# Attention with a convolutional gated unit: row-tiled scores, masks on TensorE, PSUM copies regrouped, fourth-tap product on VectorE

## The chip, the cores and the metric

The kernel runs on one core of one Trainium2 chip. The metric is the device time of one execution in microseconds (us), median of several runs; the fast runs of a kernel mostly fell within 1.5% of each other. The engines are named as the profile names them: PE is TensorE (PEld its weight loads), DVE is VectorE, ACT is ScalarE, POOL is GpSimd, SP is SyncE, which issues transfers.

## The reference

Causal attention for 8 batches, 8 heads, 576 positions and head size 64, with a decay from a cumulative sum per head, followed by a gated unit whose gate is a causal convolution of five taps.

```python
scores = scale * np.matmul(q, k.transpose(0, 1, 3, 2))
s_pos = np.maximum(s, 0.0)
cum = np.cumsum(s_pos, axis=-1)
bias = -(cum[:, :, :, None] - cum[:, :, None, :])
scores = np.where(causal, -1000000000.0, scores + np.minimum(bias, 0.0))
...                                     # softmax
x = matmul(attn, v)                     # then (batch, 576, 512)
for k in range(K):                      # K = 5
    gate_pre += conv_w[k][None, None, :] * xp[:, k:k + S, :]
gate = 1.0 / (1.0 + np.exp(-gate_pre))
val = x @ w_val
return (gate * val @ w_out)
```

## The kernel before

The work is done by head pairs, four pairs a batch, 32 in all. For each pair: transposes of Q and K on TensorE, scores, exp on ScalarE, a triangle product for the mask on VectorE, the product with V on TensorE, normalisation (`xn`), a transpose back (`xT`), five taps of the convolution, tanh, the value matmul with the gate product (`glu`), and the output matmul. The two heads of a pair share the 128 partitions; so that one matmul sees one head alone, Q is written twice, each time with the other head's half left at zero (`QZ`).

```python
def load_v(b):                                   # once a batch, GpSimd, two inputs in SBUF
    Vp = sets[b % 2]["Vp"]
    for i in range(NKB):
        ...                                      # transfer of V into vst
        nc.gpsimd.tensor_tensor(Vp[:, i], vst[:, i], w[...], ALU.mult)

def qk_transpose(b, p, which):
    ...
    if which == 0:                               # Q: two zero-padded copies, VectorE
        for hh in range(2):
            r = slice(64 * hh, 64 * hh + 64)
            nc.vector.tensor_copy(st["QZ"][hh][r, p, 0:512].rearrange(...), pt[r, :].rearrange(...))
    else:                                        # K: ScalarE
        nc.scalar.copy(st["KT"][:, p, 0:512].rearrange("d (x j) -> d x j", j=4), ...)

def scores(b, p, step):
    ...
    for (kb, q0, nq, c0) in STEPS[step]:
        for hh in range(2):
            nc.tensor.matmul(ps[:, hh, c0:c0 + nq], st["KT"][:, p, kbo[kb]:kbo[kb] + 128],
                             st["QZ"][hh][:, p, q0:q0 + nq], start=True, stop=True)
    nc.scalar.activation(out=Pt[:, :, step * 512:(step + 1) * 512], in_=ps, func=AF.Exp, scale=0.125)
    if step == 0:                                # causal mask on the diagonal blocks, VectorE
        nc.vector.tensor_tensor(dg, dg, tri..., ALU.mult)

def conv(b, c):
    nc.scalar.activation(out=gp, in_=xc[:, 4:4 + S], func=AF.Copy, scale=cwT[...])   # fourth-tap product
    for kk in range(4):
        nc.vector.scalar_tensor_tensor(gp, xc[:, kk:kk + S], cwT[...], gp, ALU.mult, ALU.add)
    nc.scalar.activation(out=th, in_=gp, func=AF.Tanh, scale=0.5)
```

GpSimd also casts Q, K and their tails to bf16 for every batch (`qkb`, `tailb`). `psav`, the PSUM tile of the product with V, has one buffer.

## Time and profile before

| before | us |
|---|---|
| median time (runs 312.5 to 314.2) | 312.95 |
| span of the profiled run | 311.1 |
| first tap of the convolution starts | 45.6 |
| from there to the last glu: VectorE busy / idle | 238.8 / 13.9 |
| last glu to the end | 12.7 |

The last rows come from VectorE's timeline (where the first tap starts and the last glu ends) and from the windows view of the stretch between. The columns of that view are the window, its length, busy time and instruction count of PE, PEld, DVE, ACT and POOL, then the granted clock, the share of the transfers and GB/s.

### The profile page before, as it was taken

To read this page: it belongs to the slowest core of one execution; us is meant where nothing else is said; L and a number is where in the kernel's file an instruction comes from. 1 tells how busy PE (TensorE), PEld (TensorE's weight loads), DVE (VectorE), ACT (ScalarE), POOL (GpSimd) and SP (SyncE) were. 2 spreads that over 40 slices of the span, in tenths; PEclk is the share of its full clock that TensorE was granted. 3 is DMA by queue.
4 is the path that set the end of the run, shared out by engine and by line. 5 is a ranking of instruction groups with operands and counts; after the bars stand their busy time and mean duration, and the time that the engine had idled before them with its cause. 6 is when DMAs were issued, how large, how long until landed. Compare 5 with 4: busy or idle time off the path is not lost. (4 is left out here: it accounts for less than half of the span.)

```text
span 311.1 us, 6044 instructions
## 1 busy us (share of the span) xinstructions
PE 215.4 (69%) x2384; PEld 151.6 (49%) x2407; DVE 259.6 (83%) x456; ACT 186.4 (60%) x256; POOL 107.0 (34%) x88
## 2 busy tenths in 40 slices
PE   0273974596747686688678875889578888767880
PEld 0152763384525564565456553666365566433440
DVE  5060689999999999999998999989988999999710
ACT  0238885587636675587666774587457778534341
POOL 8992776900690019300860059001900000000000
PEclk9996796579895999799978997799959999997998
DMA  4999999986074016676774215301100021020243
GB/s 99 261 262 325 252 291 207 316 189 223 7 174 142 2 62 192 120 202 190 221 186 127 62 67 136 84 21 67 36 0 36 19 94 43 18 104 34 84 154 96
DMA packets 71925, 40.49 MB, mean 130 GB/s; under 512 B 49808, under 2 KB 66192, under 8 KB 71888
## 3 DMA queue, kind: packets, MB, share of 16 engines
q1 hardware_dynamic: 69008, 40.00, 47.2%
q8 instruction: 21, 0.34, 0.5%
q10 hardware_dynamic: 2880, 0.01, 0.5%
q14 instruction: 16, 0.13, 0.1%
HBM read 30.57 MB, written 9.44 MB: 129 GB/s over the span
## 5 line engine op out<-in xcount | busy, mean ns | idle before, releaser
L427 DVE SCALAR_TENSOR_TENSOR gp<-xT,cwT,gp 128x576 f32<-128x576 bf16 x128 | 123.7, 967 | 3.8 <-ACT gp L425 3.6
L379 ACT ACTIVATE P<-ps 128x1024 bf16<-128x1024 f32 x96 | 96.7, 1025 | 27.1 <-PE ps L377 24.2
L377 PE MATMUL ps<-QZ,KT 128*128 128x128 bf16 (+4 forms) x512 | 75.8, 273 | 16.9 <-ACT P L379 15.1
L314 POOL CAST qkb<-qkf 128x2048 bf16<-128x2048 f32 (+2 forms) x18 | 32.9, 1843 | 98.2 <-issue 44.1
L377 PEld LDWEIGHTS <-KT 128*128 128x128 bf16 x512 | 43.4, 110 | 32.4 <-issue 22.9
L395 PE MATMUL psav<-Vp,P 128*128 128x65 bf16 x960 | 43.6, 201 | 21.0 <-DVE xn L404 18.1
L325 POOL TENSOR_TENSOR Vp<-vst,w 128x520 bf16<-128x520 f32 x40 | 55.2, 1412 | 0.0
L395 PEld LDWEIGHTS <-P 128*128 128x128 bf16 x960 | 39.5, 103 | 27.7 <-issue 16.3
L440 PE MATMUL m<-xT,wv 128*128 128x288 bf16 x256 | 46.5, 314 | 7.1 <-DVE xT L419 4.4
L450 PE MATMUL m<-wo,glu 128*128 128x512 bf16 x137 | 40.2, 388 | 13.7 <-DVE glu L442 11.8
L453 ACT COPY ot<-m 128x512 f32<-128x512 f32 (+1 forms) x40 | 23.4, 585 | 37.0 <-PE m L450 35.0
L440 PEld LDWEIGHTS <-wv 128*128 128x128 bf16 x256 | 25.7, 106 | 20.9 <-issue 5.6
L430 ACT ACTIVATE th<-gp 128x576 f32<-128x576 f32 x32 | 21.9, 684 | 21.4 <-DVE gp L427 21.4
L442 DVE SCALAR_TENSOR_TENSOR glu<-th,m 128x288 bf16<-128x288 f32 x64 | 28.6, 448 | 6.6 <-PE m L440 6.1
L346 PE MATMUL m<-ident,qkb 128*128 128x128 bf16 x256 | 28.0, 242 | 6.9 <-DVE xT L419 3.3
L350 DVE COPY QZ<-m 64x512 bf16<-64x512 bf16 x64 | 26.8, 419 | 5.1 <-PE m L346 4.4
L450 PEld LDWEIGHTS <-glu 128*128 128x128 bf16 x160 | 15.7, 99 | 27.8 <-issue 16.6
L382 DVE TENSOR_TENSOR P<-P,tri 128x1024 bf16<-128x1024 bf16 x32 | 26.9, 841 | 2.8 <-ACT P L379 2.0
L425 ACT ACTIVATE gp<-xT,cwT 128x576 f32<-128x576 bf16 x32 | 24.8, 775 | 6.8 <-DVE xT L419 6.8
L404 DVE TENSOR_TENSOR xn<-psav,recs 128x640 bf16<-128x640 f32 x32 | 26.1, 815 | 0.1
L346 PEld LDWEIGHTS <-qkb 128*128 128x128 bf16 x256 | 19.4, 108 | 12.7 <-issue 7.5
L416 DVE COPY xT<-m 128x512 bf16<-128x512 bf16 x32 | 21.4, 668 | 0.7 <-PE m L415 0.7
(50 smaller groups left out, 134.2 us busy)
## 6 DMA issues: line engine op xcount, KB each, us to landing
vst<-in_v_dram SPq DMA_DIRECT2D x32, 256.0 KB, 4.8
out_dram<-ot SPq DMA_DIRECT2D x32, 256.0 KB, 2.0
qkf<-in_q_dram SPq DMA_DIRECT2D x7, 1024.0 KB, 6.6
qkf<-in_k_dram SPq DMA_DIRECT2D x7, 1024.0 KB, 8.6
tail<-in_q_dram SPq DMA_DIRECT2D x8, 128.0 KB, 3.9
tail<-in_k_dram SPq DMA_DIRECT2D x8, 128.0 KB, 3.9
vst<-in_v_dram SPq DMA_DIRECT2D x8, 128.0 KB, 3.8
qkf<-in_moe_w_val_dram SPq DMA_DIRECT2D x1, 1024.0 KB, 6.5
```

Source lines behind the costliest of these rows:

```text
L314: nc.gpsimd.tensor_copy(t.rearrange("p j (h d) -> p h j d", h=8)[:, h0:h1], f.rearrange("p h (j d) -> p h j d", j=4)[:, h0:h1])
L325: nc.gpsimd.tensor_tensor(Vp[:, i], vst[:, i], w[:, i, b * 8:(b + 1) * 8].unsqueeze(2).to_broadcast([128, 8, 65]), ALU.mult)
L346: nc.tensor.transpose(pt[:, j * 128:(j + 1) * 128], st["qk"][which][:, j, c], ident)
L350: nc.vector.tensor_copy(st["QZ"][hh][r, p, 0:512].rearrange("d (i j r) -> d j i r", j=4, i=4), pt[r, :].rearrange("d (j i r) -> d j i r", ...
L377: nc.tensor.matmul(ps[:, hh, c0:c0 + nq], st["KT"][:, p, kbo[kb]:kbo[kb] + 128], st["QZ"][hh][:, p, q0:q0 + nq], start=True, stop=True)
L379: nc.scalar.activation(out=Pt[:, :, step * 512:(step + 1) * 512], in_=ps, func=AF.Exp, scale=0.125)
L382: nc.vector.tensor_tensor(dg, dg, tri.unsqueeze(1).unsqueeze(1).to_broadcast([128, 2, 4, 128]), ALU.mult)
L395: nc.tensor.matmul(psav[:, hh, qb * 65:qb * 65 + 65], lhsT, Vp[:, kb, 2 * p + hh, :], start=(kb == 0), stop=(kb == qb))
L427: nc.vector.scalar_tensor_tensor(gp, xc[:, kk:kk + S], cwT[:, c * 5 + kk:c * 5 + kk + 1], gp, ALU.mult, ALU.add)
L440: nc.tensor.matmul(psv, wv[:, dc, c * 128:(c + 1) * 128], st["xT"][:, dc, 4 + o:4 + o + 288], start=(dc == 0), stop=(dc == 3))
L442: nc.vector.scalar_tensor_tensor(st["glu"][:, c, o:o + 288], st["th", c][:, o:o + 288], 1.0, psv, ALU.add, ALU.mult)
L450: nc.tensor.matmul(pso, st["glu"][:, c, WIN[i]:WIN[i] + 128], wo[:, c, :], start=(c == 0), stop=(c == 3))
```

## The change

The intent is to take work from VectorE, the fullest engine. Scores become matmuls over 64 rows, one for each head, so the zero-padded second copy of Q isn't needed. The causal mask becomes matmuls that add -30000 to the scores in PSUM before the exp. Q and K of a pair leave PSUM in one ScalarE copy that also restores token order, so the later `xT` copy is dense. In exchange VectorE takes the fourth-tap product from ScalarE. Along with that the order of issue was rewritten (a queue of pieces between the scores), the first batch's casts went from GpSimd to VectorE, the casts of the two output weights from ScalarE to GpSimd, and the twenty small transfers of convolution weights became one.

```diff
 def qk_transpose(b, p):
-    if which == 0:
-        for hh in range(2):
-            nc.vector.tensor_copy(st["QZ"][hh][r, p, 0:512]..., pt[r, :]...)
-    else:
-        nc.scalar.copy(st["KT"][:, p, 0:512]..., pt...)
+    nc.scalar.copy(st["QKT"][:, :, p, 0:512].rearrange("d w (x j) -> d w x j", j=4),
+                   pt.rearrange("d w (j x) -> d w x j", j=4))

 def qk_matmul(ps, st, hh, p, k0, q0, nq, c0, **kw):
+    r = slice(64 * hh, 64 * hh + 64)
+    nc.tensor.matmul(ps[:, hh, c0:c0 + nq], st["QKT"][r, 1, p, k0:k0 + 128],
+                     st["QKT"][r, 0, p, q0:q0 + nq], **kw)

 def scores(b, p, step):
+    if step == 0:
+        for j in range(2):
+            for hh in range(2):
+                r = slice(64 * hh, 64 * hh + 64)
+                ...
+                nc.tensor.matmul(o, sel[r, j, :], f, start=False, stop=(j == 1), skip_group_check=True)
     nc.scalar.activation(out=..., in_=ps, func=AF.Exp, scale=0.125)
-    if step == 0:
-        nc.vector.tensor_tensor(dg, dg, tri..., ALU.mult)

 def x_transpose(b, p):
-    nc.vector.tensor_copy(st["xT"][:, p, 4:516].rearrange(...), pt[:, 0:512].rearrange(...))
-    nc.vector.tensor_copy(st["xT"][:, p, 516:4 + S], pt[:, 512:S])
+    nc.vector.tensor_copy(st["xT"][:, p, 4:4 + S], pt)

 def conv(b, c):
-    nc.scalar.activation(out=gp, in_=xc[:, 4:4 + S], func=AF.Copy, scale=cwT[:, c * 5 + 4:c * 5 + 5])
+    nc.vector.tensor_scalar(gp, xc[:, 4:4 + S], cwT[:, c, 4:5], None, ALU.mult)

 for src, dst, sc in ((moe_w_val, wv, 1.0), (moe_w_out, wo, 0.5)):
-    nc.scalar.activation(out=dst, in_=wt, func=AF.Copy, scale=sc)
+    nc.gpsimd.tensor_scalar(dst, wt, sc, None, ALU.mult)
```

## The prediction

> **What bounds the kernel now.** I read the page's busy table and slices first, to see which engine is full and where; then the windows, for the same thing in microseconds; then the groups kept apart by shape, for the price of each operation; then the timelines of VectorE (DVE) and GpSimd (POOL) in one place, to see why the same instruction has two prices; last the start and the end.
>
> ```profile
> PE 215.4 (69%) x2384; PEld 151.6 (49%) x2407; DVE 259.6 (83%) x456; ACT 186.4 (60%) x256; POOL 107.0 (34%) x88
> DVE  5060689999999999999998999989988999999710
> ```
>
> DVE is full from about 47 us to 296 us; nothing else is. The windows say so in microseconds (columns: window, then busy time of PE, PEld, DVE, ACT, POOL, then granted clock and DMA):
>
> ```profile
> 100.00:150.00 50.00, 37.78 (x485) 27.72 (x489) 48.44 (x92) 34.25 (x47) 14.12 (x9) 0.96 0.46 125
> 150.00:200.00 50.00, 37.68 (x399) 26.53 (x403) 47.83 (x80) 30.17 (x43) 22.12 (x15) 0.86 0.47 126
> ```
>
> DVE is busy 48 of 50 us, PE 38, ACT 30 to 34. The chain of waits agrees (DVE has the largest share, 29%). One batch of four head pairs takes 33.9 us: the same copy of the output (first block of a batch) stands in the chain at 166.15, 200.07 and 233.99. That is 8.5 us for one pair, 32 pairs in all. So what a pair costs DVE is what it costs the kernel. The prices:
>
> ```profile
> L427 DVE SCALAR_TENSOR_TENSOR gp<-xT,cwT,gp 128x576 f32<-128x576 bf16 x128 | 123.7, 967 | 3.8 <-ACT gp L425 3.6
> L442 DVE SCALAR_TENSOR_TENSOR glu<-th,m 128x288 bf16<-128x288 f32 x64 | 28.6, 448 | 6.6 <-PE m L440 6.1
> L382 DVE TENSOR_TENSOR P<-P,tri 128x1024 bf16<-128x1024 bf16 x32 | 26.9, 841 | 2.8 <-ACT P L379 2.0
> L350 DVE COPY QZ<-m 64x512 bf16<-64x512 bf16 x64 | 26.8, 419 | 5.1 <-PE m L346 4.4
> L404 DVE TENSOR_TENSOR xn<-psav,recs 128x640 bf16<-128x640 f32 x32 | 26.1, 815 | 0.1
> L416 DVE COPY xT<-m 128x512 bf16<-128x512 bf16 x32 | 21.4, 668 | 0.7 <-PE m L415 0.7
> L366 DVE TENSOR_TENSOR P<-P,tri 128x512 bf16<-128x512 bf16 x8 | 8.0, 1003 | 7.3 <-ACT P L364 7.3
> L419 DVE COPY xT<-m 128x64 bf16<-128x64 bf16 x32 | 5.7, 179 | 0.0
> ```
>
> Records of neighbours overlap by some 0.08 us, so I take the pitch in the chain in a quiet place (205 to 216 us): a tap of the convolution 0.73, glu 0.45 or 0.36, xn 0.73, mask product 0.69, the two QZ copies 0.32 and 0.43, xT 0.60 and 0.10, reciprocal 0.13. The tap's mean record is 967 ns, its median 810: it has a slow form, and the two timelines show when (start, duration):
>
> ```profile
> 184.66 2.44 DVE L427 SCALAR_TENSOR_TENSOR gp<-xT,cwT,gp 128x576 f32<-128x576 bf16 x1
> 191.28 1.60 DVE L427 SCALAR_TENSOR_TENSOR gp<-xT,cwT,gp 128x576 f32<-128x576 bf16 x1
> 192.81 0.21 DVE L403 RECIPROCAL recs<-psav 128x10 f32<-128x10 f32 x1
> ...
> 182.30 4.19 POOL L314 CAST qkb<-qkf 128x2048 bf16<-128x2048 f32 x2 [21.68 <-issue]
> 186.46 7.34 POOL L325 TENSOR_TENSOR Vp<-vst,w 128x520 bf16<-128x520 f32 x5
> ```
>
> The slow taps lie inside a burst of POOL work, once a batch.
>
> **What the Trainium skill says.** (1) "SBUF — State Buffer", Who interferes with whom: VectorE and GpSimd share one pair of ports, taken for a whole instruction; VectorE needs it with two SBUF inputs or in a two-port mode. The trace agrees: taps and mask products slow down beside POOL, xn and the PSUM copies don't, and the one-input subtraction of 64x576 at 6.04 us took 2.20 us beside a POOL memset of 2.01 us. (2) "VectorE: DVE Perf Modes", The perf-mode tier table: copies and tensor_scalar reach 2x for fp32 in SBUF, and at most 2x from PSUM. Here the final 320-element tensor_scalar took 318 ns, and a dense 512-element PSUM copy 419 ns, while the strided xT copy took 668 ns. (3) "TensorEngine Tiling (Array Packing)", Key Properties: row tiles load and multiply in parallel, but changing the tiling mode drains TensorE. No instruction of this kernel is row-tiled, so its trace cannot say. (4) "ScalarE: Activation LUTs", What ACT_TABLE_LOAD costs: 186 ns + 0.833 ns per element. The 1024-element exp here takes 1025 ns, the 512-element copies 583: agrees.
>
> **The change part by part.** All per pair, pitches in a quiet place.
>
> DVE, removed: mask product 0.69; the two QZ copies 0.75; scores4 mask and tail copies, a quarter of (0.43 + 2 x 0.28) = 0.25; the strided xT pair 0.70. Sum 2.39. Added: one dense xT copy. From 64x256 at 284 ns and 64x512 at 419 ns, 0.53 ns an element and 0.15 fixed: 0.45 record, 0.38 pitch. Fourth-tap product, bf16 to fp32 in SBUF: 576/2 cycles plus 0.15, also 0.45 record, 0.38 pitch (1x would be 0.75 record). So −1.63. Before, quiet: 4 x 0.73 + 0.81 + 0.73 + 0.13 + 2.39 = 6.98. After: 5.35.
>
> POOL's burst stays (two casts, one tail cast, five Vp products a batch). Before it cost DVE: taps 128 x (0.967 − 0.810) = 20 us, mask products 32 x (0.841 − 0.69) = 5, small ones 8 x (1.00 − 0.43) = 5: 30 us, or 0.95 a pair. The products are gone, but taps fill more of DVE's time (2.9 of 5.35 instead of 2.9 of 6.98) and the new product is a two-port instruction; I take 1.2. After: 6.55 a pair against 7.93; with its idle the old pair was 8.3 to 8.5.
>
> ACT, removed: gp product 0.775, K copy 0.583 and its tail 0.09. Added: one Q and K copy of 1024 elements, priced like an exp of that size: 1.02 on 28 of 32 pairs in the loop, 0.9, and a tail copy of 512, 0.58 / 4 = 0.15. Sum −0.40: from 186.4 / 32 = 5.8 to about 5.4.
>
> PE: scores stream 3072 columns a pair, plus a quarter of 512 for the short block. With both heads at once it is half, 1600. Masks add 256 + 512 columns (paired over heads), and 256 / 4 for the short block: 832. So 3200 becomes 2430 columns, 0.3 us less at full clock, against 190 changes between tiled and full instructions in the compiled order, 6 a pair, of an unknown price; at 0.1 us (an estimate: half the 0.2 us record of the shortest matmul) they cost 0.6. PE stays near 6 us.
>
> Start: the first exp begins at 20.01, behind POOL memsets until 14.2 and the ACT queue's twenty small transfers (its table load waits until 9.86). The change removes both and puts the first casts on DVE: first exp near 11. The conv weights now land behind some 5.5 MB (Q, K, V, two weights) at the 260 GB/s of the slices, near 23; four xn come first in DVE's order. First tap near 30, where it is 45.6 now. End: from the last glu (298.4) to the end (311.1) is 12.7 us of output blocks; the order of the last six output blocks is unchanged, so it stays.
>
> **Sum.** From the first tap: 32 x (2.92 + 0.38 + 0.38 + 0.81) = 144, 28 xn with reciprocal 24, POOL burst 7 batches x 5 = 35: 203. The same sum for before gives 247 where the trace has 255 (3% idle). Now three engines lie at 5.4, 6 and 6.55, so I expect 5 to 8% idle: 10 to 16 us. 30 + 203 + 13 + 12.7 = 259; the xn overlap partly with waits for the weights, minus 3: 256.
>
> **The rivals.** (a) PE becomes the bound: row tiles don't overlap, or mode changes drain long. Without overlap the streams are 3200 + 1664 columns, 1.0 us a pair more than with it; PE near 7, the kernel 270 to 280. For: masks add 144 matmuls; some head pairs are split by a transpose in the compiled order. Against: the two heads write different banks. (b) The port: the new product waits behind every POOL instruction, and DVE loses 2 us a pair instead of 1.2: 275. For: the 2.20 us subtraction. Against: the burst is 12 us of 28. (c) The order no longer hides latencies: psav has one buffer, and the m tiles two, read by slower copies; ACT then waits on PE and idle goes to 12%: 270. (d) The gain is larger: POOL's burst moves beside PSUM-input work, and the start is earlier: 240. (e) ACT takes over as bound; at 5.4 with the overlap of records that seems unlikely.
>
> **Range and chances.** DVE's removed work alone is 1.63 x 32 = 52 us, the start 15; contention and idle give back about 10. Range 243 to 272. For no gain over 2%, all 60 us would have to come back as waits: faster 0.97, same 0.02, slower 0.01.
>
> **What would show it.** DVE busy near 205 us; the xT copy near 450 ns and the product near 450 ns in quiet places; the Q and K copy near 1.0 us; first exp near 11 and first tap near 30 us; batch pitch near 27.5 us; last glu to end near 13. Wrong if PE is the busiest engine or waits show DVE idle for PE over 10%, if the two heads' matmuls run one after the other, or if the product's mean is over 1 us.

## More of the kernel before

The line for before:

```profile
45.60:298.40 252.80, 187.66 (x2096) 132.26 (x2118) 238.84 (x418) 159.87 (x220) 72.34 (x47) 0.89 0.40 110
```

VectorE is busy 94% of these 253 us.

## The result and the profile after

The changed kernel took 288.99 us in the median of four runs (286.0 to 290.3; the slowest counts as slow), against 312.95 us before: a ratio of 0.920, 95% interval 0.911 to 0.928. Ratios here are the mean time of one kernel's runs over that of the other's of the same rounds, so they are not quite the ratio of the medians quoted. Executions over 1.5% slower than the fastest of the same kernel are left out of the means. The kernel became 8% faster; 256 us (18%) were predicted, with a range of 243 to 272. The profiled run took 286.0 us, with a span of 284.2.

The page of the changed kernel, first the busy table and then the busy tenths of VectorE and GpSimd in 40 slices of the span:

```profile
PE 208.3 (73%) x2534; PEld 135.4 (48%) x2555; DVE 215.8 (76%) x342; ACT 175.5 (62%) x218; POOL 108.6 (38%) x87
...
DVE  4303229997999799949997799949995999999310
ACT  1389264756564867587648866795659887622250
POOL 9379976940691046602490229201810000000000
```

VectorE has lost 44 us of work but the kernel only 27. DVE's row was all 9s and 8s before. Now, from the seventh slice on, each 4, 5 and 7 in it stands where POOL's row has a 0 or a 2; only near the end, when the scores run out, is it full without POOL. The stretch from first tap to last glu, in the same columns as before:

```profile
41.93:271.70 229.77, 178.04 (x2197) 115.24 (x2218) 203.66 (x319) 150.04 (x188) 74.66 (x48) 0.93 0.47 124
```

So the span is 41.9 until the first tap, 203.7 of VectorE's work, 26.1 of its idle time, and 12.5 after the last glu. The prices, from the groups kept apart by shape (count, then busy time and mean ns of one, then idle time before them):

```profile
L439 DVE SCALAR_TENSOR_TENSOR gp<-xT,cwT,gp 128x576 f32<-128x576 bf16 x128 | 126.2, 992 | 0.6
L354 ACT COPY QKT<-m 128x1024 bf16<-128x1024 bf16 x32 | 31.4, 1019 | 5.6 <-PE m L353 5.6
L430 DVE COPY xT<-m 128x576 bf16<-128x576 bf16 x32 | 14.5, 452 | 24.0 <-PE m L429 23.0 <-PE psav L409 0.7
L437 DVE TENSOR_SCALAR gp<-xT,cwT 128x576 f32<-128x576 bf16 x32 | 24.7, 771 | 1.8
```

The dense `xT` copy and the Q and K copy cost what was predicted (0.45 and 1.02). The product has a median of 520 ns, and its mean of 771 shows the slow form beside GpSimd. It was priced at 450, so in quiet places it costs 0.07 us more than predicted. VectorE's largest new wait is for TensorE's transpose (`xT`, 23.0 us, of which 8.1 lie before the first tap).

The next lines are windows of the loop, chosen by GpSimd's timeline: in the first, third and fifth GpSimd is busy throughout, in the others it is silent.

```profile
76.80:86.60 9.80, 6.23 (x85) 4.14 (x84) 9.80 (x12) 5.36 (x6) 9.80 (x6) 0.93 0.13 29
86.60:99.30 12.70, 11.75 (x145) 7.55 (x142) 10.62 (x21) 9.37 (x11) 0.01 (x1) 0.79 0.01 1
108.80:118.40 9.60, 7.11 (x96) 4.46 (x94) 9.46 (x13) 6.62 (x9) 9.56 (x6) 1.00 0.87 248
118.40:123.80 5.40, 2.88 (x58) 2.47 (x59) 5.31 (x11) 2.78 (x5) 0.00 (x0) 1.00 1.17 240
138.80:148.70 9.90, 7.18 (x74) 4.60 (x73) 9.67 (x13) 5.61 (x7) 9.86 (x6) 0.72 0.76 254
151.00:160.60 9.60, 8.48 (x121) 5.82 (x120) 6.39 (x13) 9.36 (x12) 0.00 (x0) 1.00 0.53 103
```

Beside GpSimd VectorE is busy 28.9 of 29.3 us, TensorE 20.5 and ScalarE 17.6: VectorE alone is full. In the silent windows from 86.6 and 151.0 it is the other way: TensorE 20.2 of 22.3 us and ScalarE 18.7, VectorE 17.0. The window from 118.4 lies between: the backlog is still being worked off. In ten such windows of the loop VectorE is busy 99% beside GpSimd and 82% without it (TensorE 71% and 86%). These windows were chosen. Counted by all records from the first tap to the last glu, GpSimd works in 74.7 of the 229.8 us, and in these VectorE is idle for 1.1 us; in the other 155.1 us it is idle for 25.0 (busy 84%, TensorE 81%, ScalarE 66%). So nearly all of VectorE's idle time lies where GpSimd is silent, but over the whole silent time no engine is full: the engines wait for one another there (TensorE 14.0 us for the exps and 19.6 for VectorE's `xn` and `glu`; VectorE 23.4 us for TensorE, in the waits view of the stretch). In its steady state this kernel has two phases with different limits. The kernel before had them too, less marked: 0.5 us of its 13.9 us of idle time lay beside GpSimd.

### The profile page after: what moved, and what is told of

It is laid out like the page before. It is cut to its first block, busy times and chain, and to the rows that moved or that the text cites. A ratio compares the mean times of both kernels' runs of the same rounds, so it can differ in the third digit from the quotient of the medians.

```text
span 284.2 us, 6148 instructions
## 1 busy us (share of the span) xinstructions
PE 208.3 (73%) x2534; PEld 135.4 (48%) x2555; DVE 215.8 (76%) x342; ACT 175.5 (62%) x218; POOL 108.6 (38%) x87
## 5 line engine op out<-in xcount | busy, mean ns | idle before, releaser
L439 DVE SCALAR_TENSOR_TENSOR gp<-xT,cwT,gp 128x576 f32<-128x576 bf16 x128 | 126.2, 992 | 0.6
L332 POOL TENSOR_TENSOR Vp<-vst,w 128x520 bf16<-128x520 f32 x40 | 55.2, 1405 | 31.6 <-PE psav L409 25.9
L359 PE MATMUL ps<-QKT 64*128 64x128 bf16 (+4 forms) x576 | 49.3, 259 | 16.7 <-ACT P L397 15.1
L409 PE MATMUL psav<-Vp,P 128*128 128x65 bf16 x960 | 45.0, 201 | 11.1 <-DVE xn L418 10.9
L262 POOL CAST qkb<-qkf 128x2048 bf16<-128x2048 f32 x14 | 28.6, 2046 | 58.1 <-PE m L353 27.2
L451 PE MATMUL m<-xT,wv 128*128 128x288 bf16 x256 | 41.3, 299 | 9.0 <-ACT ot L464 6.3
L359 PEld LDWEIGHTS <-QKT 64*128 64x128 bf16 x576 | 23.6, 99 | 39.0 <-issue 31.5
L464 ACT COPY ot<-m 128x512 f32<-128x512 f32 (+1 forms) x40 | 23.3, 582 | 22.8 <-PE m L461 10.6
L354 ACT COPY QKT<-m 128x1024 bf16<-128x1024 bf16 x32 | 31.4, 1019 | 5.6 <-PE m L353 5.6
L430 DVE COPY xT<-m 128x576 bf16<-128x576 bf16 x32 | 14.5, 452 | 24.0 <-PE m L429 23.0
L353 PE MATMUL m<-ident,qkb 128*128 128x128 bf16 x256 | 22.5, 244 | 5.5 <-ACT QKT L344 2.5
L437 DVE TENSOR_SCALAR gp<-xT,cwT 128x576 f32<-128x576 bf16 x32 | 24.7, 771 | 1.8
L417 DVE RECIPROCAL recs<-psav 128x10 f32<-128x10 f32 x32 | 6.8, 212 | 15.9 <-PE psav L409 15.9
```

The source lines that it names most:

```text
L262: cast(t.rearrange("p j (h d) -> p h j d", h=8)[:, h0:h1], f.rearrange("p h (j d) -> p h j d", j=4)[:, h0:h1])
L332: nc.gpsimd.tensor_tensor(Vp[:, i], vst[:, i], w[:, i, b * 8:(b + 1) * 8].unsqueeze(2).to_broadcast([128, 8, 65]), ALU.mult)
L353: nc.tensor.transpose(pt[:, which, j * 128:(j + 1) * 128], st["qk"][which][:, j, c], ident)
L354: nc.scalar.copy(st["QKT"][:, :, p, 0:512].rearrange("d w (x j) -> d w x j", j=4), pt.rearrange("d w (j x) -> d w x j", j=4))
L359: nc.tensor.matmul(ps[:, hh, c0:c0 + nq], st["QKT"][r, 1, p, k0:k0 + 128], st["QKT"][r, 0, p, q0:q0 + nq], **kw)
L409: nc.tensor.matmul(psav[:, hh, qb * 65:qb * 65 + 65], lhsT, Vp[:, kb, 2 * p + hh, :], start=(kb == 0), stop=(kb == qb))
```

## The experiments

The first runs were chosen between these readings; the expectations call them by letters where they needed one. Theory A: GpSimd's weight casts delay the start, and that is where the gain went. Theory F: the loop has two phases, one beside GpSimd's burst (its casts and V products of a batch) where VectorE paces and one without where TensorE and ScalarE pace, so quiet work taken from VectorE turns into its idle time, while work lengthened by GpSimd is time. The supply rival: GpSimd delivers Q, K or V too late. The overlap rival: row-tiled matmuls don't run two at a time. The letters C and D mean what each expectation says beside them.

Every experiment starts from the changed kernel. The table gives the median, the ratio to the kernel before in the same rounds, and the split of the profiled run's span. Two kernels give a wrong result. One of the four of the changed kernel, one of the four of the tap-product run and the profiled one of the head-order run were slow and don't enter the ratios.

| kernel | median us | ratio to before (95%) | first tap | VectorE work | idle | end |
|---|---|---|---|---|---|---|
| before | 312.95 | 1 | 45.6 | 238.8 | 13.9 | 12.7 |
| changed | 288.99 | 0.920 (0.911 to 0.928) | 41.9 | 203.7 | 26.1 | 12.5 |
| masks back on VectorE | 306.6 | 0.978 (0.972 to 0.984) | 43.8 | 226.6 | 22.8 | 12.0 |
| tap product back on ScalarE | 287.1 | 0.916 (0.904 to 0.928) | 43.0 | 189.4 | 41.0 | 12.5 |
| weight casts on ScalarE | 288.3 | 0.928 (0.920 to 0.936) | 41.6 | 204.7 | 25.5 | 13.5 |
| x transposes earlier | 287.0 | 0.922 (0.913 to 0.931) | 33.5 | 214.6 | 24.4 | 12.0 |
| no GpSimd work from batch 2 (wrong) | 255.1 | 0.818 (0.810 to 0.826) | 42.9 | 173.4 | 24.7 | 12.5 |
| same, tap product on ScalarE (wrong) | 260.3 | 0.834 (0.829 to 0.840) | 42.7 | 162.7 | 40.4 | 12.5 |
| heads one after the other | 288.8 | 0.921 (0.914 to 0.928) | 44.3 | 203.5 | 28.7 | 12.5 |
| V products by pair, on GpSimd | 296.2 | 0.947 (0.944 to 0.951) | 44.0 | 208.8 | 29.0 | 12.6 |
| casts by the transfer | 285.6 | 0.921 (0.913 to 0.929) | 44.7 | 196.9 | 29.8 | 12.3 |
| same, transfers ahead of V products | 281.7 | 0.907 (0.900 to 0.914) | 44.9 | 194.2 | 25.7 | 12.1 |
| V products on VectorE | 282.0 | 0.907 (0.897 to 0.916) | 45.1 | 206.0 | 17.2 | 12.5 |
| casts by the transfer and V on VectorE | 268.3 | 0.863 (0.854 to 0.872) | 44.0 | 192.5 | 18.0 | 13.0 |
| combined, tap product partly on ScalarE | 259.1 | 0.834 (0.827 to 0.841) | 45.5 | 182.8 | 16.2 | 12.9 |
| combined, loop's tap product on VectorE | 263.0 | 0.843 (0.836 to 0.851) | 45.3 | 189.4 | 15.6 | 12.9 |

### Masks back on VectorE

```diff
-        for j in range(2):
-            for hh in range(2):
-                ...
-                nc.tensor.matmul(o, sel[r, j, :], f, start=False, stop=(j == 1), skip_group_check=True)
+            nc.vector.tensor_tensor(dg, dg, tri.unsqueeze(1).unsqueeze(1).to_broadcast([128, 2, 4, 128]),
+                                    ALU.mult)
```
(The same for the short block.)

> The changed kernel with the mask alone undone: no mask matmuls, the exponentials are multiplied by a triangle on VectorE as before (in token order). VectorE gets 32 x 0.69 + 8 x 0.43 = 25.5 us of quiet work, and two-input instructions that collide with GpSimd (some 8 us more); TensorE loses 144 matmuls, some 0.35 us a pair. My first sum (VectorE's work is time): slower by 26 to 34 us, 315 to 323. Theory F: slower by 8 to 20 us, 297 to 309.

It took 306.6 us, and its ratio is 0.058 above that of the changed kernel, some 18 us, as theory F expected (8 to 20). The mask product has two SBUF inputs and sits on the path from the exp to the product with V. VectorE's work grew by 22.9 us and its idle time shrank by 3.3. So most of the gain that was realised is the mask's: up to 18 of 24 us. The granted clock was 0.851 to 0.858 in all four runs, against 0.896 to 0.920 in those of the changed kernel; how much of the 18 us goes with the clock was not separated.

### Tap product back on ScalarE

```diff
-        nc.vector.tensor_scalar(gp, xc[:, 4:4 + S], cwT[:, c, 4:5], None, ALU.mult)
+        nc.scalar.activation(out=gp, in_=xc[:, 4:4 + S], func=AF.Copy, scale=cwT[:, c, 4:5])
```

> The changed kernel with the fourth-tap product back on ScalarE. It takes 24.7 us of records off VectorE (32 of 771 ns) and puts 24.8 us (32 of 775 ns) on ScalarE. Theory C (VectorE's own work still sets the pace in the loop, 10% idle apart): faster by 8 to 15 us, 274 to 281. Rival D (the loop is set by waits around TensorE's in-order queue and ScalarE, VectorE only follows): within 4 us of 289, or slower.

VectorE's work fell by 14.3 us, its idle time rose by 14.9, and the time stayed (ratio 0.916 against 0.920). That is not how an engine behaves that paces all through, as the prediction's sum has it: theory C's 274 to 281 missed.

### The start: weight casts on ScalarE, and x transposes earlier

```diff
-        nc.gpsimd.tensor_scalar(dst, wt, sc, None, ALU.mult)
+        nc.scalar.activation(out=dst, in_=wt, func=AF.Copy, scale=sc)
```

> The changed kernel with one line undone: the two weight casts back on ScalarE (1.9 us each there before) instead of GpSimd (5.37 and 5.36 us in the changed kernel's trace, from 20.9 to 31.6 us, in front of the casts of batch 1). Theory A (the late start is GpSimd's: batch 1's tail cast waits behind the weight casts, TensorE reaches its transpose before the first x transpose, so the first tap is at 41.9 us): the first tap comes at 32 to 36 us and the time falls by 5 to 9 us, to 280 to 284. Rival B (the start is set by the transfers, or whatever is won there is lost again in waits): first tap within 3 us of 41.9 and the time within 2 us of 289.

The ratio was 0.928, so no gain; the first tap came at 41.6 instead of 41.9. ScalarE's casts now stood among the first batch's exps (from 25.1 to 29.7), the fourth `xn` began at 36.3 instead of 31.6, and GpSimd's cast of the next tail ended hardly earlier (35.4 instead of 35.9), because it now waited for transfers and for a product with V. Theory A in this form fell.

The second run puts the x transpose (with the convolution behind it) ahead of the next batch's transposes in the list of pieces to be issued.

```diff
+        if n < NS:
+            f += [lambda: x_transpose(b, p)]
         if n < NS and p == 0 and b + 1 < B:
             f += [lambda: tail_transpose(b + 1)]
         ...
-        if n < NS:
-            f += [lambda: x_transpose(b, p)]
```

> The changed kernel with only the order of issue changed: the transpose of the normalised attention output and its convolution are put ahead of the tail and Q and K transposes and of the output blocks, instead of last, in each pair's list. Theory D (VectorE idles once a batch because TensorE's in-order queue reaches that transpose 3 to 5 us after its input is ready, 14.9 us of such waits after the first): these waits fall below 6 us and the time falls by 6 to 14 us, first tap also earlier. Rival C (VectorE sets the pace and the waits are slack): within 3 us of 289.

In the changed kernel the fourth `xn` was ready at 32.4, but VectorE's timeline shows that it then waited for the transpose, which stood behind transposes that waited for GpSimd's casts:

```profile
31.59 0.82 DVE L418 TENSOR_TENSOR xn<-psav,recs 128x640 bf16<-128x640 f32 x1
40.54 0.46 DVE L430 COPY xT<-m 128x576 bf16<-128x576 bf16 x1 [8.13 <-PE m L429]
```

With the transposes earlier the first tap came at 33.5, 8.4 us sooner, and the time was the same (ratio 0.922). VectorE's timeline of this run shows why: the early work ran beside the weight casts (5.4 us each) and the first burst on GpSimd.

```profile
28.69 0.46 DVE L430 COPY xT<-m 128x576 bf16<-128x576 bf16 x1 [0.21 <-PE m L429]
29.18 4.29 DVE L437 TENSOR_SCALAR gp<-xT,cwT 128x576 f32<-128x576 bf16 x1
33.39 0.20 DVE L417 RECIPROCAL recs<-psav 128x10 f32<-128x10 f32 x1
33.51 2.31 DVE L439 SCALAR_TENSOR_TENSOR gp<-xT,cwT,gp 128x576 f32<-128x576 bf16 x1
```

A product that takes 0.52 us in a quiet place took 4.29, a tap 2.31 instead of 0.81. VectorE's work grew by 10.9 us (7.7 of it in the groups of taps and product), and so the 8.4 were spent.

### No GpSimd work from batch 2 on

This kernel gives a wrong result: from batch 2 on the older batches' Q, K and V are used again, without loads, casts and V products.

```diff
+        if b >= 2:
+            st["qk"], st["tail"] = stage[b - 2]["qk"], stage[b - 2]["tail"]
+            return
 ...
+        if b >= 2:
+            return
         Vp = Vps[b % 2]
```

> Wrong result on purpose: from batch 2 on nothing is loaded, cast or multiplied on GpSimd; Q, K and V of batches 0 and 1 are used again. Everything else runs as in the changed kernel. The slow forms of the taps (128 x (992 - 812) = 23 us) and of the fourth-tap product (32 x (771 - 520) = 8 us) should go but for the part in batches 0 and 1, some 24 us of VectorE's busy time. Theory C (VectorE sets the pace): the time falls by 15 us or more, to below 274. Rival D (the order around TensorE sets it): VectorE's busy time falls by 20 us or more but the time by less than 10.

It took 255.1 us. VectorE's work fell by 30.3 us, its idle time by 1.4, and the span by 30.7: here the work counts one for one. The groups of this run show where the 30 us lay (compare the same groups of the changed kernel above):

```profile
L444 DVE SCALAR_TENSOR_TENSOR gp<-xT,cwT,gp 128x576 f32<-128x576 bf16 x128 | 103.6, 816 | 0.6
...
L442 DVE TENSOR_SCALAR gp<-xT,cwT 128x576 f32<-128x576 bf16 x32 | 16.6, 518 | 1.8
```

Taps lost 22.6 us and the product 8.1. The prediction had put 35 us on GpSimd's bursts, so its size was about right. That it was supply, GpSimd delivering too late, would show as idle time, and that fell by 1.4 us only. But the run doesn't tell GpSimd's instructions from the transfers that it also took away; the run with both casts and V products taken from GpSimd, further below, does.

### The same, with the tap product on ScalarE

> Wrong result on purpose: the kernel without GpSimd work from batch 2 on (255.1 us) with the fourth-tap product also back on ScalarE (which by itself left the changed kernel at 287.1 against 289.0). Theory F, two phases (beside a GpSimd burst VectorE paces, elsewhere TensorE and ScalarE with their waits do): without bursts there is only the second kind, so taking 17 us of quiet work (32 x 0.52) off VectorE and putting 25 on ScalarE gives nothing: 253 to 266. Rival C (VectorE paces everywhere): 240 to 247.

The edit is the tap product's, above (again wrong). Without bursts the same edit that was free in the changed kernel costs 5 us (ratio 0.834 against 0.818, intervals apart): VectorE's work fell by 10.7 us, its idle time rose by 15.7. So without bursts VectorE doesn't pace, and work put on ScalarE, or the wait for it, does count. This supports theory F's second phase, whose 253 to 266 it met.

### Heads one after the other

The two loops over heads and blocks are swapped, for scores and masks, so that neighbouring matmuls use the same half of the rows.

```diff
-        for n, (kb, q0, nq, c0) in enumerate(STEPS[step]):
-            for hh in range(2):
+        for hh in range(2):
+            for n, (kb, q0, nq, c0) in enumerate(STEPS[step]):
```

> The changed kernel with the two loops over heads and over blocks exchanged in the scores and masks, so that neighbouring matmuls use the same half of the array and cannot overlap; same instructions, same results. If row tiles overlap now, TensorE's streams grow by some 2430 columns a pair, 1.0 us at full clock, 32 us in all. Theory F (outside the bursts TensorE and ScalarE pace): slower by 10 to 25 us, 299 to 314. Rival C (VectorE paces): within 4 us of 289. If row tiles never overlapped: no change at all, and TensorE's busy time the same.

The time didn't change (ratio 0.921), so theory F's 299 to 314 missed, and the outcome is also what was expected "if row tiles never overlapped". The traces decide. Runs of eight matmuls of 128 columns on TensorE's timeline, first of the kernel before, then the changed one, then this one:

```profile
89.30 0.61 PE L377 MATMUL ps<-QZ,KT 128*128 128x128 bf16 x8
```

```profile
78.71 0.40 PE L359 MATMUL ps<-QKT 64*128 64x128 bf16 x8
```

```profile
81.50 0.41 PE L359 MATMUL ps<-QKT 64*128 64x128 bf16 x8
```

One such matmul alone has a record of some 0.2 us (its end is modelled); what the eight take beyond it halved, from 0.41 to 0.20. That a matmul over 64 rows is simply faster is ruled out by places of this run where a transpose comes between the two heads. First a 320- and a 192-column matmul of one head alone, then both heads together, four matmuls, in the same time:

```profile
116.27 0.39 PE L359 MATMUL ps<-QKT 64*128 64x320 bf16 x2
```

```profile
154.90 0.40 PE L359 MATMUL ps<-QKT 64*128 64x320 bf16 x4
```

So two matmuls of one half run one after the other (0.146 us between these starts), the halves do work side by side, and the overlap rival is out. The starts of the four also show why the order of the heads didn't matter. The program has 320 and 192 columns of the first head, then 320 and 192 of the second (the compiled program has them in this order); the records start with 320, 320, 192, 192 columns, at 0, 0.006, 0.146 and 0.153 us. The second head's first matmul didn't wait for the first head's second one, which stood before it. The edit changed the order in the program and not the order in time.

The starts also give the price of a change between tiled and full matmuls that the prediction could only estimate. In the changed kernel, where one full matmul follows another without a semaphore, the next start comes within some 0.003 us of the time that the columns of the first take (128 columns 0.055 us). At each of the 161 changes of tiling that lie at the full clock it comes at least 0.093 us later than that, and 0.095 to 0.106 where no semaphore is waited for. There are 192 changes, so by an estimate from these numbers (192 x 0.097 / 32) they take some 0.6 us of TensorE's time a pair, as the prediction had it.

### V products by head pair

If one long burst is the trouble, smaller pieces might help: four products of 650 elements into four tiles, each of which comes free with its own pair, in place of five of 520.

```diff
-            nc.gpsimd.tensor_tensor(Vp[:, i], vst[:, i], ...)
+        for p in range(4):
+            h = slice(2 * p, 2 * p + 2)
+            nc.gpsimd.tensor_tensor(Vp[p], vst[:, :, h], ..., ALU.mult)
```

> The changed kernel with GpSimd's five V products of a batch (one for each key block, 8 heads, 520 elements) replaced by four (one for each head pair, all key blocks, 650 elements), each into its own tile: the same 2600 elements, but each product can start only when its own head pair of two batches before has been used, so that the work is spread over the batch. Theory F: DVE's and TensorE's paces average out better: faster by 4 to 12 us, 277 to 285. Rival (the blocking costs the same wherever it falls): within 3 us of 289.

A miss: 296.2 us, slower than the changed kernel by some 3% (ratio 0.947). The taps' mean rose to 1045 ns. GpSimd's timeline shows that the edit hardly spread the products: in five of the seven later batches all four ran in one piece, and they waited 42.2 us for V's transfer, where the five waited 5.4. As many taps were slow (33, before 32), but a slow one took 1.72 us on average instead of 1.53, beside products of 1.55 us instead of 1.41. So the run doesn't test spread-out work, and its cause is not shown.

### Which part of the burst: casts or V products

Four runs. The casts are taken from GpSimd's arithmetic by letting the transfer convert (batch 1 and later):

```diff
+            for src, t in ((q, qb), (k, kb)):
+                for j in range(4):
+                    nc.gpsimd.dma_start(out=t[:, j].rearrange("p (h d) -> p h d", h=8),
+                                        in_=src[b, :, j:512:4, :].rearrange("h p d -> p h d"))
+            return
```

Such a transfer has to be issued by GpSimd: the Trainium skill, "DMA: Bandwidth & Descriptors", in the table of the section on SWDGE, HWDGE and iDMA, gives conversion on the way to that path alone. No run here tried another engine; the trace shows that GpSimd is now busy for 0.9 us with each of the 56 issues for Q and K.

> From batch 1 on the loads of Q, K and the tail give bf16 themselves (the transfer converts), so GpSimd's two casts of 2048 elements (about 4.2 us each) and the tail cast (about 0.9 us) go; the V products (7.3 us a batch) stay. GpSimd was busy 108.6 us, here near 40 to 45. Theory F (GpSimd's bursts lengthen VectorE's two-input work and that goes into the time one to one): the kernel without GpSimd work from batch 2 was 33 us faster; this takes away 9 of 17 us of a burst, so I expect 0.55 of it, 12 to 22 us: 266 to 276, taps with a mean near 890 ns, VectorE busy near 200 us. Rival (the gain of the kernel without loads came from the missing transfers or the missing weights of supply, not from the port): same as the changed kernel, 284 to 290.

It took 285.6 us, where 266 to 276 were expected: a miss. The waits show one reason, GpSimd's issue of the tail's transfer waiting 15.2 us for the previous batch's product with V, because in GpSimd's order it stood behind the V products. So the next run issues the transfers first:

```diff
+        if n < NS and p == 3 and b + 2 < B:
+            f += [lambda: load_qk(b + 2)]
         if n < NS and p == 3 and b + 1 < B:
             f += [lambda: load_v(b + 1)]
-        if n < NS and p == 3 and b + 2 < B:
-            f += [lambda: load_qk(b + 2)]
```

> As the run with converting transfers for Q, K and tail (285.6 us), with those transfers issued before the V products in GpSimd's queue instead of behind them (there they waited 15 us for the products' own wait on the previous batch). If that run's small gain was a matter of late loads, this one comes out at 270 to 278, with fewer waits of TensorE for Q and K. If the V products on GpSimd alone are what costs, it stays at 281 to 288, with VectorE busy near 209 us and taps near 950 ns as there.

It took 281.7 us, at the lower edge of the second expectation, with taps at a mean of 929 ns: some 4 us came from the order, and order and casts together were worth 7 us (0.907 against 0.920, intervals that overlap). The V products that stayed on GpSimd still hold most of the loss.

The other part alone, the V products on VectorE:

```diff
-            nc.gpsimd.tensor_tensor(Vp[:, i], vst[:, i],
+            (nc.vector if b else nc.gpsimd).tensor_tensor(Vp[:, i], vst[:, i],
```

> Only the V products of batch 1 to 7 on VectorE; GpSimd keeps the casts (one input, 9.3 us a batch). Theory F: takes 0.45 of the 32 us away (14) and adds 20 of VectorE's own work, part of it itself lengthened by the casts: 288 to 298. If casts with one input hinder VectorE much less than the two-input products do, it comes out at 275 to 285.

This gives the fuller engine 27 us of new work, and yet the kernel became faster (282.0; ratio 0.907 against 0.920). The groups say what was paid and what came back:

```profile
L439 DVE SCALAR_TENSOR_TENSOR gp<-xT,cwT,gp 128x576 f32<-128x576 bf16 x128 | 115.3, 908 | 0.2
...
L332 DVE TENSOR_TENSOR Vp<-vst,w 128x520 bf16<-128x520 f32 x35 | 26.9, 789 | 5.4 <-DMA vst<-in_v_dram 5.3
...
L437 DVE TENSOR_SCALAR gp<-xT,cwT 128x576 f32<-128x576 bf16 x32 | 17.2, 536 | 1.0 <-ACT P L397 0.4
```

V products cost 26.9; taps (10.9) and product (7.5) gave back 18.4 (differences of busy time to the changed kernel). VectorE's work in the stretch rose by only 2.3 us (the first V products lie before it, and records overlap) and its idle time fell by 8.9: the new work filled the quiet phase, and the burst became shorter. Here theory F's sum had counted the new work in full and the return too low; it missed by 6 us. It is the alternative of the expectation that fits, with 275 to 285.

Both together:

> As the run before it, and the V products of batch 1 to 7 on VectorE (5 of 520 elements a batch, fp32 in, some 0.65 us each, 3.3 us a batch, 20 us in the loop). GpSimd has then no instruction left in the loop but the issue of transfers. Theory F: VectorE's taps return to 810 to 830 ns and the product to near 520, that takes 32 us away and gives 20 back: 270 to 280, about the run before it. If it comes out below 266, blocking costs more than the same work done on VectorE itself; over 284, the rest of the loop is paced by what VectorE has to do.

It took 268.3 us, a ratio of 0.863, just below the 270 to 280 of theory F. The gains don't add (7 and 7 alone, 21 together by the medians): only without any burst are taps back at 809 ns. So neither half of the burst is the cause alone. The transfers are busier here than in the kernels above (0.94 of the loop, with 128-byte rows), and the taps are quick all the same, so the slow forms come from GpSimd's instructions and not from transfers. This answers the question that the run without GpSimd's work left. With that run's idle time the supply rival is out as the main cause; that part of the 8.1 us of idle time gained here is earlier supply isn't excluded.

### Combined

In addition both output weights are converted by the transfer (the factor 0.5 goes into the output copy), and the tap product goes to ScalarE in the last batch and in every second pair.

```diff
-        wt = qkf_p.tile([128, 4, DM], FP32, name="qkf")
-        nc.sync.dma_start(out=wt, in_=src.rearrange("(c p) d -> p c d", c=4))
-        nc.gpsimd.tensor_scalar(dst, wt, sc, None, ALU.mult)
+        nc.gpsimd.dma_start(out=dst, in_=src.rearrange("(c p) d -> p c d", c=4))
 ...
-        nc.scalar.copy(ot[r, :], pso[r, :])
+        nc.scalar.activation(out=ot[r, :], in_=pso[r, :], func=AF.Copy, scale=0.5)
 ...
+        if b == B - 1 or c % 2:
+            nc.scalar.activation(out=gp, in_=xc[:, 4:4 + S], func=AF.Copy, scale=cwT[:, c, 4:5])
+        else:
             nc.vector.tensor_scalar(gp, xc[:, 4:4 + S], cwT[:, c, 4:5], None, ALU.mult)
```

> As the run with converting transfers and V products on VectorE (268.3 us), and both output weights converted by the transfer too (the factor 0.5 goes into the output copy), and the fourth-tap product on ScalarE for every second pair and for the whole last batch. GpSimd then has no cast at all. Start: VectorE's 7.15 us product beside a weight cast goes, 2 to 6 us earlier. Loop: VectorE 151 of 160 us busy there, 6 x 2 x 0.52 = 6 us less of it, ScalarE 9 more (134): minus 2 to 6. Last batch: 4 x 0.52 = 2 us less on VectorE. I expect 254 to 264; 266 to 270 if VectorE no longer paces and TensorE or the transfers (busy 0.94 there) do.

It took 259.1 us and is correct: 0.834 of before, and 9% below the changed kernel by the quotient of the two ratios (0.834 / 0.920). The page of this run, busy table and VectorE's row:

```profile
PE 202.4 (79%) x2536; PEld 131.1 (51%) x2555; DVE 195.3 (76%) x359; ACT 184.8 (72%) x236; POOL 74.4 (29%) x101
...
DVE  4500404999999999999997899989978999888400
```

The deep holes in DVE's row are gone. The start isn't earlier, though (first tap 45.5; the expectation had 2 to 6 us). The granted clock in this profile is 0.98 against 0.92 in that of the changed kernel, but it doesn't explain the gain: two runs of this kernel at 0.981 and 0.922 took 259.13 and 259.16 us.

The twin keeps the tap product on VectorE in the loop and has it on ScalarE only in the last batch:

> As the combined run, with the fourth-tap product on ScalarE only in the last batch. If VectorE paces the loop, 2 to 6 us slower than the combined one (258 to 268); if ScalarE does, as fast or faster.

It took 263.0 us, and its four runs (261.2 to 265.0) lie above the four of the combined kernel (258.7 to 260.8). The intervals of the two ratios overlap, though, and the twin's slowest run had the lowest clock (0.904). So with V products on VectorE and no burst VectorE seems to pace the loop again, in part: 6.6 us less of its work came with 3.9 us less time. Where it had reserve, in the changed kernel, a whole product a pair was worth nothing.

## Why the prediction was wrong

The direction, and nearly every price, were right; the sum wasn't. Set against the trace it reads like this (spans):

| term | predicted | changed kernel | difference |
|---|---|---|---|
| until the first tap | 30 | 41.9 | +11.9 |
| VectorE's work from there to the last glu | 203 | 203.7 | +0.7 |
| its idle time in that stretch | 13 | 26.1 | +13.1 |
| last glu to the end | 12.7 | 12.5 | -0.2 |
| overlap of xn with waits for the weights | -3 | none | +3 |
| sum | 255.7 | 284.2 | +28.5 |

- **Prices and bursts: right.** Copies and VectorE's work are as predicted, the product in quiet places took 0.52 where 0.45 was expected, and GpSimd's bursts cost VectorE 30.7 us (taps 22.6, product 8.1, measured by leaving them out) where 35 stood in the sum. That VectorE's work came out within 0.7 us is in part luck: the burst's price was some 4 us too high and the product's some 2 us too low (32 x 0.07). The end was right.
- **Row tiling: right.** The streams halved, and the changes of tiling cost what was estimated (0.1 us each, 0.6 a pair). The first exp came at 13.6, not at 11.
- **The idle step failed.** "Now three engines lie at 5.4, 6 and 6.55, so I expect 5 to 8% idle": it was 11.4% of the stretch (26.1 of 229.8), and 23.4 us of it, 10.2%, were waits for TensorE: the prediction's own sign of being wrong, "DVE idle for PE over 10%", came true. The averages hid two phases. Of VectorE's work a large part falls into GpSimd's bursts, in which VectorE alone paces and the others wait; outside of them no engine is full, and VectorE waits in its turn. A sum of VectorE's work with a small allowance is the time only if it paces in both. The tap-product run shows the second phase (14.3 us less work, 14.9 more idle), the run without GpSimd the first (30.3 less work, 30.7 less time). Rival (c) had the size, 12% idle and 270, but named other causes (one psav buffer, two m tiles), and rival (b) had the port, but as work and not as idle time. Neither was carried far enough, and the range left out their sum.
- **The calibration hid it.** The working takes before as 247 of 255 us, "3% idle". Measured over the stretch itself it is 238.8 of 252.8 us (the 255 doesn't come out of the trace), 5.5%: about 8 us of what the 32 pairs cost lay ahead of the first tap or in overlaps. So before already had twice the idle time that the step started from.
- **The start step failed, in size and in kind.** "First tap near 30": it came at 41.9, because transposes for the next batch, waiting for casts behind two weight casts on GpSimd, stood ahead of the x transposes in TensorE's order. The working saw the loads and left out that the weight casts had moved to GpSimd. But an earlier first tap wasn't time either: brought to 33.5, it cost 10.9 us more work beside GpSimd. Start and burst are not independent terms, as the sum has them.
- **The masks** were priced as VectorE time (0.69 us a pair and more beside GpSimd); undoing them alone cost 18 us (at a lower clock), so they make most of the gain. That the product and the regrouped copies together gave so little fits the same two phases; a run with the copies alone undone was not made, and their share stays open.

What stays open besides: why the smaller V products were slower; why casts and V products cost more together than the two alone, beyond the argument that each keeps a burst in place; and how much of the silent phase is TensorE's, ScalarE's or the waits between them.

## What to carry to other kernels

When an engine is at 80 or 90% on average, cut the steady state into windows by what a neighbour that shares its port is doing, before summing: in this kernel, taking work from the engine was worth time only where it paced. Look at what the neighbour could give up first. Here giving the fullest engine the neighbour's V products, which is more work for it, made the kernel 7 us faster, and 21 us with the neighbour's casts gone too. A start that was made earlier, into the neighbour's burst, gained nothing.

## What the Trainium skill lacked or had wrong

- "SBUF — State Buffer", Who interferes with whom: its rule agrees with what was seen (taps and the product slow down, xn and PSUM copies don't), but it gives no size for a stream of instructions. Here V products alone on GpSimd (busy 52.3 us, casts by the transfer) left the taps at a mean of 958 ns, casts alone (35.3 us, those of Q, K and tails) at 908, against 816 without either from batch 2 on; both together gave 992. The order of issue matters too: with the transfers ahead of the V products it was 929 instead of 958.
- The same page expects issue of transfers by GpSimd to compete with VectorE's two-port modes. It gives a price for the transfer that waits, and none for VectorE. With 70 converting transfers issued by GpSimd and no other work of its in the loop, none of the 128 taps was slow, but four of the 32 products took 0.58, 0.67, 0.72 and 0.91 us where the others took 0.50 to 0.52. They are four of the five that ran while one issue for Q or K followed another: an effect that is seen, but small, 0.8 us in all.
- "TensorEngine Tiling (Array Packing)", Key Properties: it names a drain at each change of tiling mode, without a price, and that different tiles run in parallel, without saying whether they must alternate in the program. Here a change cost 0.095 to 0.106 us between the starts of two matmuls, and the order of the heads made no difference (0.40 and 0.41 us for eight matmuls), because a matmul of one half started before one of the other half that stood ahead of it.
- "DMA: Bandwidth & Descriptors": the table of measured sizes in its section on bandwidth has no line for converting transfers that scatter rows of 128 bytes. Here they kept the transfers busy for 0.94 of the loop at 115 GB/s, against 0.54 at 138 GB/s with plain loads and casts on GpSimd, and each issue took GpSimd 0.9 us.
